# Attention scheduled by a planner: GpSimd shifts in half batches, other ring sizes, three-bank score phases

## The chip, the cores and the metric

One core of one Trainium2 chip. The metric is device time in microseconds of one execution; a run's time is the median of several executions. PE is TensorE, DVE VectorE, ACT ScalarE, POOL GpSimd, SP the queue that issues transfers.

## The reference, cut to what matters

```python
x = A_x                                   # 1 x 2048 x 512, bf16
xn = _layernorm(x)
# A: 32 query heads of 16, one key head and one value head
scores = einsum("bhqd,bkd->bhqk", q, k) * 16 ** -0.5
p = softmax(scores);  o = einsum("bhqk,bkd->bhqd", p, v);  s = o @ wo
# B: a gated layer
g = silu(silu(xn @ w1) @ w2)
return x + s * g
```

There are 32 x 2048 x 2048 scores. They come out of PE as 2,048 score slots of 128 keys x 512 queries, one PSUM bank each. Every slot must go through an exponential before PE multiplies it with the values.

## The kernel before

The kernel is a list scheduler. It simulates the five engines with planned durations, gives each engine a fixed order of instructions, and emits that order with semaphore waits. The chip may be late or early against the plan, but the order stays.

A slot leaves its bank in one of two ways. ACT takes it through `Exp`, one or two banks at a time. Or DVE takes it: four such slots make a *batch*. DVE writes each slot as a 16-bit integer whose bits, read as bf16, approximate the exponential (one *eviction*); then three *shifts* add a constant to the whole batch, and PE adds the four versions with different weights. A shift is an integer add from SBUF to SBUF: GpSimd does it, or, when many are open or a group of heads is closing, DVE.

PE alternates between *score phases* (tiles of 32 rows, two to four slots into two to four banks) and *column runs* (tiles of 32 columns: value products and the dense layers).

```python
T_P, T_SH, T_TR, T_AF = 600.0, 600.0, 630.0, 64.3      # planned ns; T_SH: a shift on Vector
T_P64, DV_MIN, T_LIB = 1035.0, 4, 300.0                # T_P64: a shift on GpSimd
...
NEAR, AHEAD = 24, 0.6
NPA, PRESS = 26, 20                                    # slots of the exp ring
WIDE, NMIN, EARLY = 2, 2, 200.0                        # NMIN: banks a score phase waits for
...
    def locked(self, eng, ports):                      # the planner's model of the shared port
        if ports != 2 or eng not in self.lock:
            return 0.0
        return self.lock[PO if eng == DV else DV]
...
    def run_engine(self, e, handle):                   # what is emitted: a fixed order with waits
        for op in self.order[e]:
            for d in op.waits:
                handle.wait_ge(d.sem, d.val)
            h = op.emit(handle)
...
    OB = 6
    BANKS = (0, 1, 2, 3, 4, 5, 7)
    NDB, NDS = 7, 6                                    # batch tiles, shift tiles
...
        def s_phase_ready():
            g = a_group(0)
            if g >= NG:
                return None
            if not all(slot_ok(g, i) for i in range(4) if left[g, i]):
                return None
            bt = bank_times()
            spare = JOB_SPARE if st["job"] < len(jobs) and not [a for a in active if not a.fixed] and jobs[st["job"]].pace <= progress() + 1e-9 else 0
            n = len(bt) - spare
            if n < 1:
                return None
            need = act_need() - 437.0
            n = min(n, 4)
            while n > NMIN and bt[n - 1][0] > need:
                n -= 1
            if n < NMIN and need > pl.clk[PE] or n < 1:
                return None
...
                bt.P[i] = pl.add(Task(DV, T_P, lambda v, b=b, i=i, bb=bt.b: v.tensor_scalar(
                    db_sb[:, bb, i * NQ:(i + 1) * NQ], bank(b), 128.0 * LOG2E, 128.0 * (SHIFT_BETA + 127.0),
                    op0=ALU.mult, op1=ALU.add), [("ps", b)], [("Db", bt.b, i)], 0, on_place=placed))
...
        def split(bt, s, j):
            whole = {}

            def placed(pop, eng):
                other = DV if eng == PO else PO
                pl.tasks[other].remove(whole[other])
                shifts.remove(whole)
                release(bt)
                for i in range(4):
                    kt = bt.slots[i]
                    pvq[bt.g][i].append((pop, v_lhs(j, bt.g, kt), ds_sb[:, s, i * NQ:(i + 1) * NQ].bitcast(BF16),
                                         [("Ds", s, i)] + v_reads(j, kt), ("s", s)))

            reads = [("Db", bt.b, i) for i in range(4)]
            step = int(SHIFT[j - 1])
            words = step | step << 16 | step << 32 | step << 48
            urgent = lambda: bt.g == st["gO"] and nleft[bt.g] <= CLOSING
            whole[DV] = pl.add(Task(DV, T_SH, lambda v: v.tensor_scalar(
                ds_sb[:, s, :], db_sb[:, bt.b, :], SHIFT[j - 1], 1.0, op0=ALU.add, op1=ALU.mult),
                reads, ds_keys(s), lambda: URGENT if urgent() else 6, list(bt.P.values()),
                on_place=lambda op: placed(op, DV), ports=2,
                gate=lambda: urgent() or len(shifts) >= DV_MIN))
            whole[PO] = pl.add(Task(PO, T_P64, lambda g: g.int64_add(
                ds_sb[:, s, :].bitcast(U64), db_sb[:, bt.b, :].bitcast(U64), words),
                reads, ds_keys(s), lambda: 5 if urgent() else 6, list(bt.P.values()),
                on_place=lambda op: placed(op, PO), ports=2))
            shifts.append(whole)
...
        # closing a group: the multiply with two SBUF inputs
            t3 = pl.add(Task(DV, 332.0, lambda v: v.tensor_tensor(
                o3[:, :, val:val + DH], f3[:, :, val:val + DH],
                rcp_sb[:, k, :].unsqueeze(2).to_broadcast([P, NQ // 32, DH]), ALU.mult),
                [("F", k), ("rcp", k)], [("otr", oi % 2, e)], 3, [t2, t2_task.get(oi - 2)], ports=2))
```

The softmax here doesn't subtract the row's maximum and nothing guards it: scores larger than these inputs give would overflow.

## Time and profile before

| | |
|---|---|
| time | 694.91 us (694.9 to 695.0) |
| span, granted TensorE clock | 693.2 us, 0.999 |
| GpSimd shifts, DVE shifts | 489 whole batches, 36 |
| PE's floor, PE's waiting | 656.3 us, 28.4 us |

A line of the groups reads: source line, engine, operation, output<-input, count | busy us, mean ns of one | idle time of the engine just before them, and what ended it. The timeline gives start, duration, engine, line, operation, count. Two figures come from the instruction order together with the starts in the trace: *PE's floor*, the sum over its phases and runs of what each takes from start to next start when nothing holds it, and *PE's waiting*, what it takes beyond that. The prediction shows how they come about.

### The profile page before, as it was taken

How to read it: one execution, taken by the hardware profiler on the slowest of the kernel's cores; microseconds unless marked ns; L12 is line 12 of the kernel's file. 1: busy time of each engine (PE TensorE's matmuls, PEld its weight loads, DVE VectorE, ACT ScalarE, POOL GpSimd, SP SyncE). 2: the span in 40 equal slices, each digit the busy share in tenths (PEclk: the TensorE clock that was granted, in tenths of full speed). 3: DMA queues.
4: the chain of work that ended last, by engine and by line, in shares of the span. 5: the costliest groups of instructions: out<-in, count | busy, mean ns of one | idle time of the engine just before them, and what ended most of it. 6: DMA issues, size and time to landing. Idle time of an engine off the chain costs nothing.

```text
span 693.2 us, 20821 instructions
## 1 busy us (share of the span) xinstructions
PE 670.8 (97%) x8843; PEld 193.8 (28%) x8843; DVE 627.9 (91%) x1088; ACT 667.4 (96%) x827; POOL 519.5 (75%) x500
## 2 busy tenths in 40 slices
PE   8899999999999999999999999999999999999995
PEld 4422222222222222222222222222222222222221
DVE  9889989989998999989998999989899988999994
ACT  4899999999999999999999999999999999999994
POOL 2067887797897778877698676788789677888891
PEclk9999999999999999999999999999999999999999
DMA  9310000000000000000000100000000000000000
GB/s 302 127 18 1 3 2 2 1 3 2 2 2 17 18 32 2 2 2 2 1 2 2 32 18 17 1 2 3 2 2 1 17 18 24 9 2 2 2 2 31
DMA packets 11435, 12.64 MB, mean 18 GB/s; under 512 B 1808, under 2 KB 10768, under 8 KB 11344
## 3 DMA queue, kind: packets, MB, share of 16 engines
q1 hardware_dynamic: 10288, 11.28, 5.1%
q8 instruction: 71, 1.16, 0.7%
q10 hardware_dynamic: 1056, 0.03, 0.1%
q14 instruction: 20, 0.16, 0.1%
HBM read 8.95 MB, written 2.10 MB: 16 GB/s over the span
## 4 chain that ended last, share of the span: by engine, by line
PE 62%; ACT 24%; DVE 12%; issue 1%; ACTq 0%; DVEq 0%
PE ps L1079 25%; ACT pa_sb L1341 23%; PE ps L776 21%; PE ps L466 15%; DVE db_sb L962 5%; DVE ds_sb L1014 2%; ACT t_sb L588 1%; DVE stats_sb L413 1%; DVE f_sb L1096 1%; DVE ob_sb L643 1%; DVE u_sb L590 0%; DVE otr_sb L1100 0%; DVE xn_sb L442 0%; DVE fin_sb L640 0%; DVE xnT_sb L493 0%
## 5 line engine op out<-in xcount | busy, mean ns | idle before, releaser
L1341 ACT ACTIVATE pa_sb<-ps 128x1024 bf16<-128x1024 f32 (+1 forms) x748 | 639.7, 980 | 7.4 <-PE ps L776 6.3
L1019 POOL INT64_ADD ds_sb<-db_sb x489 | 515.5, 1072 | 158.9 <-DVE db_sb L962 102.9
L962 DVE TENSOR_SCALAR db_sb<-ps 128x512 uint16<-128x512 f32 x700 | 449.9, 682 | 44.1 <-PE ps L776 40.0
L776 PE MATMUL ps<-qt_sb,kt_sb 32*128 32x512 bf16 x2048 | 257.4, 384 | 9.1 <-DVE db_sb L962 4.0
L1079 PE MATMUL ps<-ds_sb,v_sb 128*32 128x512 bf16 x2100 | 265.1, 383 | 0.2
L1079 PE MATMUL ps<-pa_sb,v_sb 128*32 128x512 bf16 x1348 | 242.8, 383 | 1.8 <-DVE ds_sb L1014 1.0
L1079 PE MATMUL ps<-db_sb,v_sb 128*32 128x512 bf16 x700 | 171.0, 383 | 2.8 <-DVE f_sb L1096 2.8
L776 PEld LDWEIGHTS ps<-qt_sb,kt_sb 32*128 32x128 bf16 x2048 | 63.9, 91 | 281.6 <-ACT pa_sb L1341 145.8
L1079 PEld LDWEIGHTS ps<-ds_sb,v_sb 128*32 128x32 bf16 x2100 | 65.9, 95 | 60.7 <-issue 40.0
L1079 PEld LDWEIGHTS ps<-pa_sb,v_sb 128*32 128x32 bf16 x1348 | 61.2, 95 | 45.1 <-issue 23.6
L466 PE MATMUL ps<-xnT_sb,w_sb 128*32 128x512 bf16 x896 | 73.1, 384 | 0.2 <-DVE db_sb L962 0.2
L466 PE MATMUL ps<-w_sb,u_sb 128*32 128x512 bf16 x896 | 69.6, 384 | 0.0
L1079 PEld LDWEIGHTS ps<-db_sb,v_sb 128*32 128x32 bf16 x700 | 42.6, 95 | 25.8 <-issue 13.3
L588 ACT ACTIVATE t_sb<-ps 128x512 bf16<-128x512 f32 x72 | 46.3, 643 | 0.0
L590 DVE SCALAR_TENSOR_TENSOR u_sb<-t_sb,ps 128x512 bf16<-128x512 bf16 x56 | 38.1, 681 | 4.5 <-ACT t_sb L588 4.0
L1014 DVE TENSOR_SCALAR ds_sb<-db_sb 128x2048 uint16<-128x2048 uint16 x36 | 37.3, 1039 | 0.1
L1096 DVE STREAM_TRANSPOSE f_sb<-ps 128x512 f32<-128x512 f32 x32 | 22.7, 708 | 7.5 <-PE ps L1079 7.4
L466 PEld LDWEIGHTS ps<-xnT_sb,w_sb 128*32 128x32 bf16 x896 | 16.7, 94 | 25.0 <-issue 18.3
L466 PEld LDWEIGHTS ps<-w_sb,u_sb 128*32 128x32 bf16 x896 | 16.2, 94 | 26.3 <-issue 22.8
L466 PE MATMUL ps<-wo_sb,on_sb 128*32 128x512 bf16 x256 | 20.4, 383 | 0.1
L466 PE MATMUL ps<-xnT_sb,wq_sb 128*32 128x512 bf16 x256 | 20.3, 383 | 0.0
L1100 DVE TENSOR_TENSOR otr_sb<-f_sb,rcp_sb 128x256 bf16<-128x256 f32 x32 | 19.0, 595 | 0.2
(53 smaller groups left out, 153.3 us busy)
## 6 DMA issues: line engine op xcount, KB each, us to landing
w_sb<-in_B_w_dram SPq DMA_DIRECT2D x2, 1792.0 KB, 13.1
xr_sb<-in_A_x_dram SPq DMA_DIRECT2D x16, 128.0 KB, 2.6
out_dram<-ob_sb SPq DMA_DIRECT2D x16, 128.0 KB, 1.7
ds_sb<-in_A_x_dram SPq DMA_DIRECT2D x3, 512.0 KB, 7.2
ds_sb<-in_A_x_dram SPq DMA_DIRECT2D x4, 128.0 KB, 2.6
wq_sb<-in_A_wq_dram SPq DMA_DIRECT2D x1, 512.0 KB, 5.2
wo_sb<-in_A_wo_dram SPq DMA_DIRECT2D x1, 512.0 KB, 16.0
kt_sb<-kt_sb SPq DMA_DIRECT2D x4, 64.0 KB, 2.3
```

The source lines that it names most:

```text
L413: ts_ = pl.add(Task(DV, 593.0, lambda v, t=t: v.bn_stats(stats_sb[:, t, :], x_tile(t)), [xkey(t)], [("st", t)], 1 + j, gate=(lambda: q_don ...
L466: last = h.matmul(bank(b)[32 * j:32 * (j + 1), 0:n], lhsT=lhs(j), rhs=rhs, start=start, stop=stop, tile_position=(0, 32 * j), skip_group_c ...
L588: t1 = Task(AC, 490.0, lambda a: a.activation(t_sb[:, k, :], src, ACT.Tanh, scale=scale), [held], [("t", k)], 0, [t0])
L590: t2 = Task(DV, T_P, lambda v: v.scalar_tensor_tensor(out=dst, in0=t_sb[:, k, :], scalar=1.0, in1=src, op0=ALU.add, op1=ALU.mult), [held, ...
L776: return pe.matmul(bank(b), lhsT=kt_sb[32 * i:32 * i + 32, g % 2, kt * P:(kt + 1) * P], rhs=qt_sb[32 * i:32 * i + 32, (g // 2) % NQR, :], ...
L962: bt.P[i] = pl.add(Task(DV, T_P, lambda v, b=b, i=i, bb=bt.b: v.tensor_scalar(db_sb[:, bb, i * NQ:(i + 1) * NQ], bank(b), 128.0 * LOG2E, 1 ...
L1014: whole[DV] = pl.add(Task(DV, T_SH, lambda v: v.tensor_scalar(ds_sb[:, s, :], db_sb[:, bt.b, :], SHIFT[j - 1], 1.0, op0=ALU.add, op1=ALU.m ...
L1019: whole[PO] = pl.add(Task(PO, T_P64, lambda g: g.int64_add(ds_sb[:, s, :].bitcast(U64), db_sb[:, bt.b, :].bitcast(U64), words), reads, ds_ ...
L1079: h = pe.matmul(bank(OB)[32 * i:32 * (i + 1), :], lhsT=lhs, rhs=rhs, start=s0, stop=s1, tile_position=(0, 32 * i), skip_group_check=True)
L1096: t1 = pl.add(Task(DV, T_TR, lambda v: v.transpose(f_sb[:, k, :], bank(OB)), [("ps", OB)], [("F", k)], 1, [norm.get(("m", g - 2))]))
L1100: t3 = pl.add(Task(DV, 332.0, lambda v: v.tensor_tensor(o3[:, :, val:val + DH], f3[:, :, val:val + DH], rcp_sb[:, k, :].unsqueeze(2).to_br ...
L1341: op = pl.place(AC, 0.8333 * NQ * n + T_AF, lambda a: a.activation(pa_sb[:, s * NQ:(s + n) * NQ].rearrange("p (b n) -> p b n", n=NQ), ps3[ ...
```

## The change

It means to feed PE more evenly. GpSimd's adds are cut into halves of two slots, so that PE can start on the first half earlier; the shift ring grows from 6 to 8 tiles, and the exp ring shrinks from 26 to 22 slots (its limit `PRESS` from 20 to 16) and the batch ring from 7 to 6 tiles to pay for it; a phase waits for three banks and takes no two slots in one row group (the 32 rows of PE that a slot's tile uses). `NEAR`, below called the *closing limit*, falls from 24 to 12: with no more value products than that still to do, a group counts as closing. The planned 545 ns for a half add stands in `T_P64`. The source line numbers of the changed kernel are higher by 3 to 14: L1019 becomes L1032, L1014 L1026, L1100 L1114, L1341 L1355.

```diff
--- before.py
+++ after.py
@@ -20,7 +20,8 @@
 
 
 T_P, T_SH, T_TR, T_AF = 600.0, 600.0, 630.0, 64.3
-T_P64, DV_MIN, T_LIB = 1035.0, 4, 300.0
+T_P64, DV_MIN, T_LIB = 545.0, 4, 300.0
+NPIECE = 2
 RSQRT_M = float(0x5F1FFFF9)
 RSQRT_C = ((-0.703952253, 0.703952253 * 2.38924456), (-0.5, 1.5))
 
@@ -37,7 +38,7 @@
 ENGINES = (PE, AC, DV, PO, SP)
 MM = 216.0
 BLG = 0
-NEAR, AHEAD = 24, 0.6
+NEAR, AHEAD = 12, 0.6
 SWITCH, SKEW = 105.0, 10.0
 INF = float("inf")
 DVE_LIMIT = 4000.0
@@ -48,10 +49,12 @@
 LOW_USE, HIGH_USE, USE_WIN = 0.55, 0.8, 3000.0
 S_TOL = 30.0
 CLOSING, URGENT = 3, 1.5
-NPA, PRESS = 26, 20
+NPA, PRESS = 22, 16
+NDB, NDS = 6, 8
+STOL4 = 0.0
 START_Z, START_H = 8, 14
 EVAC = ()
-WIDE, NMIN, EARLY = 2, 2, 200.0
+WIDE, NMIN, EARLY = 2, 3, 200.0
 ONE_LIMIT = 2500.0
 A_LOW, JOB_SPARE = 1000.0, 0
 
@@ -293,7 +296,7 @@
 
     OB = 6
     BANKS = (0, 1, 2, 3, 4, 5, 7)
-    NDB, NDS = 7, 6
+
     NQR, NON = 4, 2 * NOC
 
     with ExitStack() as es:
@@ -809,28 +812,28 @@
             if not free:
                 return None
             bt = Job()
-            bt.g, bt.slots, bt.b, bt.P, bt.nsh, bt.left = g, {}, free[0], {}, 0, K + 3
+            bt.g, bt.slots, bt.b, bt.P, bt.nsh, bt.left = g, {}, free[0], {}, 0, 4 * K
             return bt
 
         def pick_a(n, avoid):
             res = []
-            used = set()
+            used = set(avoid)
             g = a_group(0)
             st["gA"] = g
-            for gg in (g, g + 1):
-                if gg >= NG:
-                    break
-                order = sorted(range(4), key=lambda i: (i in avoid and gg == g, -a_left(gg, i), i))
-                again = True
-                while len(res) < n and again:
-                    again = False
-                    for i in order:
-                        if len(res) < n and a_left(gg, i) > 0 and (i not in used or len(used) == 4 or gg == g and nleft[gg] <= 4):
-                            if not slot_ok(gg, i):
-                                return None if not res else res
-                            res.append((gg, i, take(gg, i)))
-                            used.add(i)
-                            again = True
+            for strict in (True, False):
+                for gg in (g, g + 1):
+                    if gg >= NG:
+                        break
+                    again = True
+                    while len(res) < n and again:
+                        again = False
+                        for i in sorted(range(4), key=lambda i: (-a_left(gg, i), i)):
+                            if len(res) < n and a_left(gg, i) > 0 and (i not in used or not strict and not res):
+                                if not slot_ok(gg, i):
+                                    return None if not res else res
+                                res.append((gg, i, take(gg, i)))
+                                used.add(i)
+                                again = True
             return res
 
         class Unit:
@@ -852,7 +855,7 @@
                 return None
             need = act_need() - 437.0
             n = min(n, 4)
-            while n > NMIN and bt[n - 1][0] > need:
+            while n > NMIN and bt[n - 1][0] > need + STOL4:
                 n -= 1
             if n < NMIN and need > pl.clk[PE] or n < 1:
                 return None
@@ -992,20 +995,29 @@
 
         shifts = []
 
-        shifts = []
-
         def split(bt, s, j):
-            whole = {}
-
-            def placed(pop, eng):
-                other = DV if eng == PO else PO
-                pl.tasks[other].remove(whole[other])
-                shifts.remove(whole)
-                release(bt)
-                for i in range(4):
+            whole = {"po": []}
+            width = 4 // NPIECE
+
+            def ready(pop, slots):
+                for i in slots:
+                    release(bt)
                     kt = bt.slots[i]
                     pvq[bt.g][i].append((pop, v_lhs(j, bt.g, kt), ds_sb[:, s, i * NQ:(i + 1) * NQ].bitcast(BF16),
                                          [("Ds", s, i)] + v_reads(j, kt), ("s", s)))
+
+            def placed_dv(pop):
+                for t in whole["po"]:
+                    pl.tasks[PO].remove(t)
+                shifts.remove(whole)
+                ready(pop, range(4))
+
+            def placed_po(pop, k):
+                if whole[DV] is not None:
+                    pl.tasks[DV].remove(whole[DV])
+                    whole[DV] = None
+                    shifts.remove(whole)
+                ready(pop, range(k * width, (k + 1) * width))
 
             reads = [("Db", bt.b, i) for i in range(4)]
             step = int(SHIFT[j - 1])
@@ -1014,12 +1026,14 @@
             whole[DV] = pl.add(Task(DV, T_SH, lambda v: v.tensor_scalar(
                 ds_sb[:, s, :], db_sb[:, bt.b, :], SHIFT[j - 1], 1.0, op0=ALU.add, op1=ALU.mult),
                 reads, ds_keys(s), lambda: URGENT if urgent() else 6, list(bt.P.values()),
-                on_place=lambda op: placed(op, DV), ports=2,
-                gate=lambda: urgent() or len(shifts) >= DV_MIN))
-            whole[PO] = pl.add(Task(PO, T_P64, lambda g: g.int64_add(
-                ds_sb[:, s, :].bitcast(U64), db_sb[:, bt.b, :].bitcast(U64), words),
-                reads, ds_keys(s), lambda: 5 if urgent() else 6, list(bt.P.values()),
-                on_place=lambda op: placed(op, PO), ports=2))
+                on_place=placed_dv, ports=2, gate=lambda: urgent() or len(shifts) >= DV_MIN))
+            for k in range(NPIECE):
+                cols = slice(k * width * NQ, (k + 1) * width * NQ)
+                whole["po"].append(pl.add(Task(PO, T_P64, lambda g, cols=cols: g.int64_add(
+                    ds_sb[:, s, cols].bitcast(U64), db_sb[:, bt.b, cols].bitcast(U64), words),
+                    reads[k * width:(k + 1) * width], ds_keys(s)[k * width:(k + 1) * width],
+                    lambda: 5 if urgent() else 6, list(bt.P.values()),
+                    on_place=lambda op, k=k: placed_po(op, k), ports=2)))
             shifts.append(whole)
 
         x_free = [False]
```

## The prediction

> **What bounds the kernel now.** I read the page first. Its busy shares put three engines near the end of their time:
>
> ```profile
> PE 670.8 (97%) x8843; PEld 193.8 (28%) x8843; DVE 627.9 (91%) x1088; ACT 667.4 (96%) x827; POOL 519.5 (75%) x500
> ...
> PE 62%; ACT 24%; DVE 12%; issue 1%; ACTq 0%; DVEq 0%
> ```
>
> PE and ACT are both "full", and the chain that ended last runs through PE for 62% of the span and through ACT for 24%. But busy is no measure of work, because a record that overlaps its neighbour is busy whether or not the engine waited inside. So I looked next at starts, in the timeline. ACT alone:
>
> ```profile
> 301.65 15.93 ACT L1341 ACTIVATE pa_sb<-ps 128x1024 bf16<-128x1024 f32 x17
> 317.44 0.63 ACT L588 ACTIVATE t_sb<-ps 128x512 bf16<-128x512 f32 x1
> 317.92 2.90 ACT L1341 ACTIVATE pa_sb<-ps 128x1024 bf16<-128x1024 f32 x3
> ```
>
> 17 exps of two banks take 15.79 us to the next start: 0.929 each. Over the trace, start to next start, a two-bank exp needs 0.904 at least and a one-bank activation 0.477. ACT's least work is therefore 600 x 0.904 + 148 x 0.477 + 72 x 0.477 (the gates) = 647.3 us; it actually spreads over 670.0. ACT has 22.7 us of hidden waiting although its row says 96%. Now PE:
>
> ```profile
> 310.55 0.39 PE L776 MATMUL ps<-qt_sb,kt_sb 32*128 32x512 bf16 x3
> 310.87 0.61 PE L466 MATMUL ps<-w_sb,u_sb 128*32 128x512 bf16 x8
> 311.42 0.39 PE L776 MATMUL ps<-qt_sb,kt_sb 32*128 32x512 bf16 x3
> 311.74 0.62 PE L466 MATMUL ps<-w_sb,u_sb 128*32 128x512 bf16 x8
> ```
>
> The reader is to see the alternation: a score phase (32-row tiles) of three slots lasts 0.32 us to the next start, whatever its slots (medians 0.318, 0.321, 0.325 for two, three, four), and a run of column-tiled matmuls 0.55 for 8, 0.764 for 12, 0.980 for 16: 0.216 for each round of four and 0.116 once. The instruction order gives the counts: 649 score phases (101 of two slots, 347 of three, 198 of four, three odd ones), 643 column runs with 1,677 rounds. PE's floor: phases 211.8; runs 643 x 0.116 + 1,677 x 0.216 less 2.8 for half-wide fillers = 434.0; full-array prologue 10.5; together 656.3 us. The time is then 2.3 (before the first matmul) + 656.3 + 28.4 (PE waiting) + 6.2 (after the last) + 1.7 (measured time over span) = 694.9. PE is the bound; of its 28.4 us of waiting 11.0 lie in the first 50 us and the last 20, and 17.4 between (13.9 a phase waiting for a bank, 3.5 a run waiting for an operand).
>
> ```profile
> PEld ps L776 <- ACT pa_sb L1341: 145.8, 348, 0.8
> PEld ps L776 <- DVE db_sb L962: 104.1, 227, 1.2
> ...
> PEld ps L1079 <- POOL ds_sb L1019: 12.1, 53, 0.4
> ```
>
> These waits name who frees the banks: ACT most often, DVE next; GpSimd's shifts hardly hold anything. Weight loads run ahead of matmuls, so most of these sums is not lost time. Where PE really waits, the chain in order of time shows a group being closed on DVE:
>
> ```profile
> 152.02 0.73 DVE f_sb L1096
> ...
> 153.06 0.80 DVE otr_sb L1100
> 153.85 1.44 DVE ds_sb L1014
> 155.30 0.62 DVE on_sb L1107
> 155.92 0.59 DVE db_sb L962
> ```
>
> An urgent shift of 1.44 us and a normalising multiply of 0.80 stand in front of the eviction that PE needs. The groups:
>
> ```profile
> L1019 POOL INT64_ADD ds_sb<-db_sb x489 | 515.5, 1072 | 158.9 <-DVE db_sb L962 102.9 <-PE ps L1079 55.2
> L962 DVE TENSOR_SCALAR db_sb<-ps 128x512 uint16<-128x512 f32 x700 | 449.9, 682 | 44.1 <-PE ps L776 40.0 <-POOL ds_sb L1019 0.4
> L1014 DVE TENSOR_SCALAR ds_sb<-db_sb 128x2048 uint16<-128x2048 uint16 x36 | 37.3, 1039 | 0.1
> L1100 DVE TENSOR_TENSOR otr_sb<-f_sb,rcp_sb 128x256 bf16<-128x256 f32 x32 | 19.0, 595 | 0.2
> ```
>
> **What the Trainium skill says.** SBUF — State Buffer, Who interferes with whom: a Vector instruction in a 2-port mode, or with two SBUF inputs, and a GpSimd instruction exclude each other for the whole instruction; the second blocks fully. The trace agrees: the same DVE shift takes 683 ns at its shortest and 1,602 at its longest, the multiply 415 and 1,256, the excess being near one GpSimd add (1,015 start to start, 1,039 alone). TensorEngine Tiling (Array Packing), Key Properties: changing the tiling mode drains the engine; agrees, as 0.105 and 0.116 us above the streaming time per change. ScalarE: Activation LUTs, What ACT_TABLE_LOAD costs: 0.833 ns per element plus a fixed part. Agrees: (904 - 477)/512 = 0.834, and 50 ns fixed from start to start. GPSIMD Engine Reference, Instruction dispatch: each instruction pays tens of cycles of software dispatch. A half add therefore costs somewhat more than half; no row of this kernel shows it.
>
> **The change part by part.** The order of instructions of both kernels:
> - *Batches.* 180 instead of 175 batches of four slots go to DVE plus shifts; ACT loses 20 slots: 600 -> 632 two-bank exps, 148 -> 64 single ones. ACT's floor: 632 x 0.904 + 136 x 0.477 = 636.2, that is -11.1. Each moved slot needs four value matmuls instead of one: +60, or 15 rounds; fillers +16.
> - *Phases.* 648 instead of 649, but 549 of three and 97 of four; none of two. So asking for three banks saves no changes of mode: the twos vanish together with half of the fours. It makes each phase one pair for ACT and one slot for DVE, which is why single exps vanish. Phases with two slots in a row group (0.533 instead of 0.321): 14 before, two after. Phases in all: 208.8, -2.9.
> - *Rounds.* 1,682 against 1,677: 19 more by matmul count, but 14 fewer wasted on partly filled rounds. Runs: 644 x 0.116 + 1,682 x 0.216 - 3.2 = 434.8, +0.8. PE's floor: 654.1, -2.2.
> - *DVE.* +20 evictions x 0.643 = +12.9; shifts 36 -> 15, -21 x 1.036 = -21.8. The wait for GpSimd, on average 0.36 for a shift (1,039 - 683) and 0.18 for a multiply (595 - 415), should halve with adds of half length: 15 x 0.18 + 32 x 0.09 = -5.6. DVE: about -14.
> - *GpSimd.* 489 whole adds become 1,050 halves. The changed kernel plans 545 ns for one; its old plan of 1,035 for a whole was right within 0.5% of the trace, so I take 545: 572 us in the 639 us in which GpSimd has work, 90% instead of 78%. It lies beside PE's work.
> - *Rings.* Exp ring 26 -> 22 slots, shift ring 6 -> 8 tiles: less cushion between exp and PE, more between shifts and PE. I count nothing for either.
>
> What reaches PE: floor -2.2. Of the 17.4 us of waiting in the middle: the chain has 1.7% = 11.8 us on DVE shifts, 21/36 of that is 6.9, and I count half as real, -3.5, since the chain then moves to PE; half of the lock's 5.6, -2.8. I add 1.5 for tighter shift supply and 0.5 for the start, where the fillers hint at more idle. Sum: 2.3 + 654.1 + 11.5 + (17.4 - 3.5 - 2.8 + 1.5 = 12.6) + 6.2 + 1.7 = 688.4 us, -0.9%.
>
> **The rivals.** (1) *ACT is the bound.* For: 96% busy, and it holds most banks. Then the time falls by ACT's 11.1 to 683.8, more if singles wasted more. Against: its own 22.7 us of hidden waiting, and PE's floor 9 us above its own before and 18 after. (2) *GpSimd becomes the bound.* The smallest add on the page's engine (one word, at load) took 189 ns; a line through it and 1,039 gives a half at 613, less 24 of overlap 589, and 1,050 x 0.589 = 618 us of 639: shifts late, runs waiting for operands, 695 to 712. Against: a first call is likely dearer than the rest. (3) *All waiting in the middle goes,* since phases become regular: 675.8. Against: closing a group still needs its transpose before the next group's values can start, 32 times. (4) *Three banks come later than two:* PE holds phases back with a smaller exp ring, waiting stays at 17.4 or grows by 5: 693 to 698.
>
> **Range and chances.** Rival 1 or half of rival 3 gives the low end, 682.5; rival 4 the high, 696. Faster by over 2% (below 681.0) asks for two thirds of the middle's waiting to go: 0.10. Slower by over 2% (above 708.8) asks for rival 2 in full: 0.04. Else 0.86.
>
> **What would show it.** Right: score phases near 0.321 and runs of 8 at 0.548 as before; two-bank exps at 0.904 or above with ACT's share of busy falling; the DVE shift's mean below 900 and the multiply's below 530; GpSimd's mean near 545 and some 85 to 92% busy; PE waiting between 50 and 670 us near 12. Wrong: GpSimd above 580 and 95% busy with PE waiting for shifts; PE waiting unchanged (the DVE closings did not matter); or a total below 682 with waiting under 6 (regularity mattered most).

## The result, and the profile after

The changed kernel takes **737.57 us** (737.42 to 737.76, four executions) against 694.94 us for the kernel before in the same rounds: 1.0613 times as long (95% interval 1.0595 to 1.0632). A ratio is the mean time of one kernel's fast runs over that of the other's of the same rounds, so not quite the ratio of the medians. The prediction of 688.4 us, and its range, were wrong.

First the page of the changed kernel, its busy shares and the chain by engine, then the row of the granted TensorE clock in 40 slices, then what the cores view says of clock and span:

```profile
PE 683.9 (93%) x8919; PEld 195.0 (26%) x8919; DVE 659.9 (90%) x1087; ACT 662.5 (90%) x775; POOL 632.1 (86%) x1061
...
PE 47%; ACT 26%; DVE 21%; issue 3%; DMA 1%; POOL 0%; SPq 0%; ACTq 0%; DVEq 0%
```

```profile
PEclk9999999999999999998998999989989999989999
```

```profile
core 0: 736.0 us, clock 0.968
```

PE and ACT lose share, DVE's part of the chain grows from 12% to 21%, and, what no row of the kernel before hinted at, the clock is below full in several slices. In the clock records it is at one half in eight stretches of 3.4 or 6.8 us, 44.4 us in all, the first 50 us and the tail after the last matmul left out. The kernel before has none there.

The groups, each shape apart:

```profile
L1032 POOL INT64_ADD ds_sb<-db_sb x1050 | 628.2, 621 | 90.9 <-DVE db_sb L965 61.2 <-PE ps L1093 28.7
...
L1114 DVE TENSOR_TENSOR otr_sb<-f_sb,rcp_sb 128x256 bf16<-128x256 f32 x32 | 42.5, 1329 | 0.1
...
L1026 DVE TENSOR_SCALAR ds_sb<-db_sb 128x2048 uint16<-128x2048 uint16 x15 | 26.0, 1735 | 0.0
```

A half add takes 621 ns (587 from start to start), not 545. And the two DVE instructions that share a port with GpSimd, which were to wait half as long, wait far longer: the multiply 1,329 on average against 595, the shift 1,735 against 1,039. What the views by tile and line give as least, median and longest, for the multiply before and after, then for the shift after:

```profile
L1100 DVE TENSOR_TENSOR otr_sb<-f_sb,rcp_sb x32: 415/434/1256, 50.2 to 685.3; 128x256 bf16<-128x256 f32 x32
```

```profile
L1114 DVE TENSOR_TENSOR otr_sb<-f_sb,rcp_sb x32: 409/714/6111, 59.6 to 728.1; 128x256 bf16<-128x256 f32 x32
```

```profile
L1026 DVE TENSOR_SCALAR ds_sb<-db_sb x15: 685/1053/6436, 42.5 to 718.6; 128x2048 uint16<-128x2048 uint16 x15
```

The medians are harmless. A few instructions take 2.5 to 6.4 us. One of them in the timelines of DVE, GpSimd, PE and ACT:

```profile
337.79 5.18 DVE L1114 TENSOR_TENSOR otr_sb<-f_sb,rcp_sb 128x256 bf16<-128x256 f32 x1
342.90 0.68 DVE L965 TENSOR_SCALAR db_sb<-ps 128x512 uint16<-128x512 f32 x1
```

```profile
336.80 5.90 POOL L1032 INT64_ADD ds_sb<-db_sb  x10
```

```profile
343.72 0.61 PE L779 MATMUL ps<-qt_sb,kt_sb 32*128 32x512 bf16 x3 [4.31 <-DVE db_sb L965]
344.26 0.62 PE L469 MATMUL ps<-xnT_sb,wq_sb 128*32 128x512 bf16 x4
```

```profile
344.38 1.02 ACT L1355 ACTIVATE pa_sb<-ps 128x1024 bf16<-128x1024 f32 x1 [4.34 <-PE ps L779]
```

The multiply starts at 337.79 while GpSimd is in a run of 48 adds without a pause, in the course of the 40th; the line of GpSimd shows the last ten. It ends at 342.97, just after the last of them, at 342.70. Behind it, in DVE's order, stands the eviction that frees PE's bank: PE idles 4.31 us, ACT 4.34. And PE comes back slow: 0.54 us from the start of the score phase to the next run, where 0.32 was the rule. The windows around it (columns: length, then busy us of PE, its weight loads, DVE, ACT and GpSimd, then the granted clock) show this:

```profile
335.00:339.00 4.00, 3.96 (x56) 1.04 (x57) 4.00 (x6) 3.90 (x5) 4.00 (x8) 1.00 0.02 4
339.00:343.70 4.70, 0.41 (x8) 0.01 (x1) 4.70 (x3) 1.03 (x2) 3.70 (x7) 0.73 0.00 0
343.70:350.00 6.30, 6.28 (x61) 1.35 (x61) 5.11 (x9) 4.21 (x5) 4.01 (x7) 0.66 0.00 0
```

Of the numbers after the stretch the fourth is DVE's busy time: DVE is "busy" all through its wait, which is why its 90% tells nothing.

Sorted by size, PE's waiting of 72.8 us in the changed kernel is: 10.7 at the two ends, 34.4 in ten stalls of over 1 us, 15.6 in the stretches at half clock, and 12.2 in everything else. Nine of the ten stalls begin within some 2 us of one of the nine DVE instructions that take over 2 us, and each of these nine ends within 0.6 us after the last add of a run. The waits say the same, and that shifts coming late to PE are not it (12.1 us before, 13.4 after):

```profile
PE ps L779 <- DVE db_sb L965: 36.3, 20, 5.1
...
PEld ps L1093 <- POOL ds_sb L1032: 13.4, 57, 0.5
```

### The profile page after: what moved, and what is told of

Same layout as the page of the kernel before. It is cut to its first block, busy times and chain, and to the rows that moved or that the text cites. A ratio compares the mean times of both kernels' runs of the same rounds, so it can differ in the third digit from the quotient of the medians.

```text
span 736.0 us, 21675 instructions
## 1 busy us (share of the span) xinstructions
PE 683.9 (93%) x8919; PEld 195.0 (26%) x8919; DVE 659.9 (90%) x1087; ACT 662.5 (90%) x775; POOL 632.1 (86%) x1061
## 4 chain that ended last, share of the span: by engine, by line
PE 47%; ACT 26%; DVE 21%; issue 3%; DMA 1%; POOL 0%; SPq 0%; ACTq 0%; DVEq 0%
ACT pa_sb L1355 25%; PE ps L1093 19%; PE ps L779 17%; PE ps L469 11%; DVE db_sb L965 11%; DVE otr_sb L1114 3%; DVE ds_sb L1026 2%; ACT t_sb L591 2%; DVE u_sb L593 1%; DMA ds_sb<-in_A_x_dram 1%; DVE stats_sb L416 1%; DVE f_sb L1110 1%; DVE ob_sb L646 0%; POOL ds_sb L1032 0%; SPq L363 0%
## 5 line engine op out<-in xcount | busy, mean ns | idle before, releaser
L1032 POOL INT64_ADD ds_sb<-db_sb x1050 | 628.2, 621 | 90.9 <-DVE db_sb L965 61.2
L1355 ACT ACTIVATE pa_sb<-ps 128x1024 bf16<-128x1024 f32 (+1 forms) x696 | 632.4, 998 | 54.9 <-PE ps L779 52.9
L965 DVE TENSOR_SCALAR db_sb<-ps 128x512 uint16<-128x512 f32 x720 | 468.9, 682 | 57.7 <-PE ps L779 54.0
L1093 PE MATMUL ps<-ds_sb,v_sb 128*32 128x512 bf16 x2160 | 280.0, 392 | 0.0
L1093 PE MATMUL ps<-db_sb,v_sb 128*32 128x512 bf16 x720 | 182.5, 389 | 0.8 <-DVE f_sb L1110 0.6
L1093 PEld LDWEIGHTS ps<-ds_sb,v_sb 128*32 128x32 bf16 x2160 | 70.9, 96 | 64.6 <-issue 42.8
L469 PE MATMUL ps<-w_sb,u_sb 128*32 128x512 bf16 x896 | 75.7, 397 | 0.0
L1093 PEld LDWEIGHTS ps<-db_sb,v_sb 128*32 128x32 bf16 x720 | 45.1, 96 | 22.2 <-issue 13.4
L591 ACT ACTIVATE t_sb<-ps 128x512 bf16<-128x512 f32 x72 | 43.7, 607 | 0.2 <-PE ps L469 0.2
L1114 DVE TENSOR_TENSOR otr_sb<-f_sb,rcp_sb 128x256 bf16<-128x256 f32 x32 | 42.5, 1329 | 0.1
L1026 DVE TENSOR_SCALAR ds_sb<-db_sb 128x2048 uint16<-128x2048 uint16 x15 | 26.0, 1735 | 0.0
```

Of the source, the lines that this page charges most:

```text
L469: last = h.matmul(bank(b)[32 * j:32 * (j + 1), 0:n], lhsT=lhs(j), rhs=rhs, start=start, stop=stop, tile_position=(0, 32 * j), skip_group_c ...
L591: t1 = Task(AC, 490.0, lambda a: a.activation(t_sb[:, k, :], src, ACT.Tanh, scale=scale), [held], [("t", k)], 0, [t0])
L1032: whole["po"].append(pl.add(Task(PO, T_P64, lambda g, cols=cols: g.int64_add(ds_sb[:, s, cols].bitcast(U64), db_sb[:, bt.b, cols].bitcast( ...
L1093: h = pe.matmul(bank(OB)[32 * i:32 * (i + 1), :], lhsT=lhs, rhs=rhs, start=s0, stop=s1, tile_position=(0, 32 * i), skip_group_check=True)
L1114: t3 = pl.add(Task(DV, 332.0, lambda v: v.tensor_tensor(o3[:, :, val:val + DH], f3[:, :, val:val + DH], rcp_sb[:, k, :].unsqueeze(2).to_br ...
L1355: op = pl.place(AC, 0.8333 * NQ * n + T_AF, lambda a: a.activation(pa_sb[:, s * NQ:(s + n) * NQ].rearrange("p (b n) -> p b n", n=NQ), ps3[ ...
```

## The experiments

Three theories. **A**, the starved port: when GpSimd's adds follow one another without a pause for long, a DVE instruction that needs the shared port is not let in at the end of an add but waits for the end of the run. The halves bring long runs because they are planned too short: GpSimd falls behind, finds all its inputs ready, and never pauses. **B**, GpSimd's throughput: 1,050 x 0.587 is 616 us of work, and that alone makes everything late. **C**, the rings or the rules for phases cost the time.

"Waits over 2 us" below counts the multiplies, the shifts and the residual sums on DVE. The "longest run" is of adds each of which starts before the record of the one before it ends. It goes on when a DVE instruction was let in between two adds. "Half clock" leaves out the first 50 us and the tail after the last matmul.

| kernel | time us | ratio | GpSimd adds | longest run | waits over 2 us | half clock us | PE floor | PE waiting |
|---|---|---|---|---|---|---|---|---|
| before | 694.9 | 1 | 489 whole | 18 | 0 | 0 | 656.3 | 28.4 |
| the change | 737.6 | 1.0613 | 1,050 half | 62 | 9 | 44.4 | 654.1 | 72.8 |
| e1 pause every 8 | 702.6 | 1.0105 | 1,050 half | 8 | 0 | 6.8 | 654.1 | 37.6 |
| e7 pause every 24 | 709.9 | 1.0186 | 1,050 half | 24 | 3 | 17.1 | 654.1 | 44.8 |
| e5 wait, no pause | 735.7 | 1.0579 | 1,050 half | 70 | 8 | 44.4 | 654.1 | 71.2 |
| e2 planned at 600 | 707.2 | 1.0183 | 984 half | 40 | 3 | 13.7 | 652.7 | 48.4 |
| e6 both | 697.5 | 1.0030 | 984 half | 8 | 0 | 0 | 652.7 | 34.1 |
| e4 halves alone | 711.1 | 1.0230 | 936 half | 61 | 1 | 6.8 | 657.8 | 42.4 |
| e3 all but halves | 692.8 | 0.9964 | 524 whole | 15 | 0 | 0 | 654.7 | 26.3 |
| e8 phase rules alone | 694.0 | 0.9982 | 502 whole | 16 | 0 | 0 | 649.6 | 32.7 |
| e9 rings alone | 693.8 | 0.9975 | 502 whole | 18 | 0 | 0 | 661.4 | 21.6 |
| e10 e3 with 24 exp slots | 688.4 | 0.9906 | 522 whole | 25 | 1 | 3.4 | 650.6 | 26.4 |

All these results are correct ones. The floor, the waiting, the runs and the waits are of the one profiled execution of each kernel; e2's took 711.8 us, the longest of its four.

### e1: a pause at every eighth add

The order of every engine is that of the changed kernel; one wait is added to every eighth add.

```diff
     def finalize(self, new_sem):
+        adds = self.order[PO]
+        for k in range(len(adds) - 1, 12, -EVERY):       # EVERY = 8
+            adds[k].deps.append(adds[k - 1])
         for e in ENGINES:
```

> The changed kernel, same order on every engine; only every eighth GpSimd add also waits for the end of the add before it (131 breaks). Theory A (starved port: in long unbroken runs of adds a Vector instruction with two SBUF inputs or in a 2-port mode does not get the port and waits 2 to 6 us): those waits fall below 2 us at most, the mean of the normalising multiply from 1,329 to below 700 ns, and the time falls to 700 to 718 us although GpSimd has some 15 us more to do. Theory B (GpSimd's throughput alone, 1,050 adds at 0.586): the time stays or rises, 735 to 755. Theory C (the rings and phase rules are what costs): no change, 733 to 742.

Measured: 702.63 us (702.35 to 702.95), interval of the ratio 1.009 to 1.012. The groups of this kernel (its lines are four higher):

```profile
L1036 POOL INT64_ADD ds_sb<-db_sb x1050 | 632.0, 622 | 52.1 <-DVE db_sb L969 38.0 <-PE ps L1097 1.2
...
L1118 DVE TENSOR_TENSOR otr_sb<-f_sb,rcp_sb 128x256 bf16<-128x256 f32 x32 | 19.7, 616 | 0.1
...
L1030 DVE TENSOR_SCALAR ds_sb<-db_sb 128x2048 uint16<-128x2048 uint16 x15 | 14.3, 952 | 0.0
```

GpSimd has the same adds of the same length plus 131 pauses, so more to do, and the kernel is 35 us faster. The multiply's mean is 616 instead of 1,329, with 894 at most. A holds; B as the main cause falls. What remains above the kernel before looks like B's share, though no run takes it apart: PE waits 25.8 us for GpSimd's shifts in the weight loads' row of the waits (13.4 in the changed kernel), and DVE's evictions wait 5.8 us (0.4) for batch tiles that late adds still read:

```profile
PEld ps L1097 <- POOL ds_sb L1036: 25.8, 83, 1.5
...
DVE db_sb L969 <- POOL ds_sb L1036: 5.8, 9, 2.7
```

### e5: as many waits, but no pause

```diff
-            adds[k].deps.append(adds[k - 1])
+            adds[k].deps.append(adds[k - 4])
```

> As e1_break8, with as many waits at the same adds, but each for the add four before, which is long done: a wait without a pause. If the pause is what lets the Vector engine in (theory A), nothing is gained: 730 to 745 us and waits of over 4 us. If it is the waiting instruction as such that opens the port, 700 to 708 as e1_break8.

Measured: 735.66 us (731.75 to 739.91), ratio 1.0579 (1.0533 to 1.0624). The groups:

```profile
L1036 POOL INT64_ADD ds_sb<-db_sb x1050 | 629.4, 620 | 88.1 <-DVE db_sb L969 64.0 <-PE ps L1097 23.3
...
L1118 DVE TENSOR_TENSOR otr_sb<-f_sb,rcp_sb 128x256 bf16<-128x256 f32 x32 | 46.2, 1443 | 0.1
```

Not the wait as an instruction opens the port but the gap it makes when its add has not yet ended. The longest multiply takes 6,164 ns, as in the changed kernel.

### e7: a pause at every 24th add

The edit is that of e1 with `EVERY = 24`.

> As e1_break8 with a pause at every 24th add. In the changed kernel the Vector engine lost from about the 12th add of a run on, so A expects it between: 708 to 728 us, longest wait at the port 3 to 6 us but fewer of them than the nine over 2 us of the changed kernel. B: 730 to 742.

Measured: 709.90 us (705.16 to 710.21), ratio 1.0186 (1.0148 to 1.0225). Between e1 and the changed kernel, with three waits over 2 us, the longest 4,049 ns. The dose works in the right direction.

### m1 and m2: the port by itself

Two measuring kernels write zeros. Their outputs are wrong, which doesn't matter for the times. Each was executed once. GpSimd issues a run of adds with no wait inside; one DVE instruction waits for the n-th add of the run and then needs the port.

```diff
+for i in range(total):                        # GpSimd: 48 adds of 256 words or 36 of 512
+    g.int64_add(dst[...], src[...], 1).then_inc(sp, 1)
...
+v.wait_ge(sp, base + p)                       # DVE: released by the p-th add
+v.tensor_tensor(vc[:], va[:], vb[:], ALU.add).then_inc(sv, 1)
```

> A measurement alone, with a wrong result on purpose (it writes zeros). First GpSimd adds of 32, 64, 128, 256 and 512 eight-byte words, ten each: I expect start to start a straight line with 0.586 us at 256 and 1.015 at 512, so some 0.157 fixed and 1.68 ns a word. Then unbroken runs of 48 half adds or 36 whole adds, and one Vector instruction (a sum of two SBUF inputs, or a 16-bit shift in a 2-port mode) released by the 2nd, 5th, 8th, 12th, 16th, 24th or 32nd add of the run, twice each. Theory A as I hold it (adds that follow one another without a pause let the Vector instruction in only while the run is young, whatever their size): released by the 2nd or 5th it waits one or two adds, released by the 24th or 32nd it waits to the end of the run, 5 us or more, with halves and with wholes. Theory A2 (only short adds starve it): with wholes it waits at most two adds at any place. Theory A3 (it takes a loaded memory or something else of the kernel): at most two adds everywhere.

The length of an add, start to start, from m1's trace (medians of nine; a word is 8 bytes):

| words | 32 | 64 | 128 | 256 (half) | 512 (whole) |
|---|---|---|---|---|---|
| ns | 211 | 268 | 375 | 588 | 1,015 |

That is (1,015 - 211) / 480 = 1.675 ns a word and 158 ns for each instruction. Two halves cost 2 x 588 - 1,015 = 161 ns more than a whole. The 545 in the plan was too low, and the prediction's "proportional plus a little" with it; the straight line of the prediction's second rival gave 589.

How long the sum of two SBUF inputs took on DVE, released by the p-th add (both trials agree within 7 ns, but for the whole adds at 32, whose second trial started later and took 3.8):

| released by add | 2 | 5 | 8 | 12 | 16 | 24 | 32 |
|---|---|---|---|---|---|---|---|
| halves, us | 0.76 | 0.76 | 0.76 | 0.76 | 0.76 | 14.29 | 9.58 |
| wholes, us | 1.19 | 1.19 | 1.19 | 1.19 | 1.19 | 12.35 | 4.23 |

The 16-bit shift on DVE behaves the same (1.03 and 1.45 up to the 16th; 14.56 and 12.62 at the 24th). Early in a run DVE waits for one add; late in a run it waits for the end of the run. Wholes starve it as halves do, and with nothing else running, so A2 and A3 fall.

> A measurement alone, with a wrong result on purpose. Runs of 48 adds of 256 or 128 words and a Vector sum of two SBUF inputs released by the 15th to the 24th add. From m1 the Vector engine loses from some add between the 17th and the 24th on; if the number of adds counts and not their time, the edge is at the same number for both sizes; if time counts (between 9.4 and 14.1 us), the short adds still let it in at the 24th. Two Vector instructions, at the 12th and again at the 24th to 36th: if a granted port starts the count afresh, the second waits one add when it comes within some 20 adds of the first, so at the 24th and 28th, not at the 36th. A pause (wait for the add just before) in front of the 17th: arrivals at the 20th to 30th wait one add, that at the 42nd may lose again. A wait for a long-done add at the same place: as without, so the 24th and 30th lose.

m2 puts the arrivals closer. Its DVE timeline: released by the 15th, 16th, 17th and 18th half add of 48, then by the 15th and 16th of 48 adds of 128 words:

```profile
17.18 0.75 DVE L70 TENSOR_TENSOR vc_sb<-va_sb,vb_sb 128x512 bf16<-128x512 bf16 x1 [9.36 <-POOL dst_sb L81]
46.28 19.00 DVE L70 TENSOR_TENSOR vc_sb<-va_sb,vb_sb 128x512 bf16<-128x512 bf16 x1 [28.35 <-POOL dst_sb L81]
75.58 18.41 DVE L70 TENSOR_TENSOR vc_sb<-va_sb,vb_sb 128x512 bf16<-128x512 bf16 x1 [10.30 <-POOL dst_sb L81]
104.88 17.82 DVE L70 TENSOR_TENSOR vc_sb<-va_sb,vb_sb 128x512 bf16<-128x512 bf16 x1 [10.89 <-POOL dst_sb L81]
...
301.20 0.55 DVE L70 TENSOR_TENSOR vc_sb<-va_sb,vb_sb 128x512 bf16<-128x512 bf16 x1 [5.93 <-POOL dst_sb L81]
319.86 8.52 DVE L70 TENSOR_TENSOR vc_sb<-va_sb,vb_sb 128x512 bf16<-128x512 bf16 x1 [18.11 <-POOL dst_sb L81]
```

The edge is sharp and lies at the same place for both sizes, between the 15th and the 16th add here and past the 16th in m1: it is the number of adds that counts, not their time. So cutting the adds brings the edge nearer in time: 16 halves take 9.4 us, 16 wholes 16.2. A grant starts the count afresh: after one at the 12th, arrivals at the 24th and 28th take 0.76 us, those at the 32nd and 36th 9.58 and 6.82. So does a pause in front of the 17th add (a gap of 97 ns in the records): arrivals at the 20th, 24th and 30th take 0.76, those at the 36th and 42nd 7.23 and 3.70. A wait for a long-done add at the same place does nothing: 16.64, 14.29 and 10.76 us at the 20th, 24th and 30th. Released by the 20th, with the pause and with the idle wait:

```profile
606.20 0.76 DVE L70 TENSOR_TENSOR vc_sb<-va_sb,vb_sb 128x512 bf16<-128x512 bf16 x1 [12.19 <-POOL dst_sb L81]
...
749.67 16.64 DVE L70 TENSOR_TENSOR vc_sb<-va_sb,vb_sb 128x512 bf16<-128x512 bf16 x1 [12.07 <-POOL dst_sb L81]
```

The expectation that a second arrival would be let in within "some 20 adds" was close: the edge lies between 16 and 20 adds after the first. One thing does not fit a wait to the end of the run: behind adds of 128 words the starved instruction got in at about the 38th or 39th of 48. That is left open, and so is the mechanism that makes the edge.

The traces of the twelve kernels above show the same edge under load. Take every multiply, shift and residual sum that came in a run with at least three adds still to follow, and count the adds since the last pause or since the last of these instructions was let in, the add then running included. Of the 304 that came by the 17th add, none took over 1 us more than its shortest time in the kernel before; of the 39 that came at the 18th or later, 25 did. All 25 instructions of over 2 us in these kernels came at the 18th or later and ended within 0.6 us after the run's last add. This is also why e4 has a run of 61 and only one such wait: instructions let in on the way started the count again.

### e2 and e6: an honest plan, without and with pauses

```diff
-T_P64, DV_MIN, T_LIB = 545.0, 4, 300.0
+T_P64, DV_MIN, T_LIB = 600.0, 4, 300.0
```

e6 adds the edit of e1 to it.

> The changed kernel, scheduled with 600 ns for a half add in place of 545, so that the plan is honest about the 586 measured: 984 half adds and 33 Vector shifts instead of 1,050 and 15. A and B: GpSimd keeps up and pauses again, 688 to 700 us, longest wait of a Vector shift or multiply below 2 us. C: the rings and phase rules are still there, so above 710.

> The honest plan of e2 with the pauses of e1. A: no wait at the port over 2 us, PE's waiting near the 26 to 30 us of the kernels with whole adds, 690 to 697 us. B: the pauses cost GpSimd 14 us, so no better than e2's 707.

Measured: e2 707.20 us (706.11 to 711.82), ratio 1.0183 (1.0147 to 1.022), which misses A's expectation of 688 to 700; e6 697.54 us (697.25 to 698.12), ratio 1.003 (1.0015 to 1.0045), just above A's 697, with 34.1 us of waiting where A expected 26 to 30. B's expectation for e6 fails too: the pauses gained. In e2 GpSimd still makes runs of up to 40 adds, and three DVE instructions wait over 2 us, the longest 4,502 ns. So being on plan does not by itself break the runs. The four times make a table: with the plan of 545, 737.6 without pauses and 702.6 with them; with 600, 707.2 and 697.5. The pauses are worth 35.0 and 9.7 us, the plan 30.4 and 5.1 (the other plan also brings another order and 18 more shifts on DVE). The two overlap: a GpSimd that is behind pauses less by itself.

### e3 and e4: the halves against the rest

e3 takes the change with whole adds; e4 takes the halves, planned at 545, into the old rings, rules and limits.

```diff
 e3, against the change
-T_P64, DV_MIN, T_LIB = 545.0, 4, 300.0
-NPIECE = 2
+T_P64, DV_MIN, T_LIB = 1035.0, 4, 300.0
+NPIECE = 1
 e4, against the change (and the old choice of slots for ACT)
-NEAR, AHEAD = 12, 0.6
+NEAR, AHEAD = 24, 0.6
-NPA, PRESS = 22, 16
-NDB, NDS = 6, 8
+NPA, PRESS = 26, 20
+NDB, NDS = 7, 6
-WIDE, NMIN, EARLY = 2, 3, 200.0
+WIDE, NMIN, EARLY = 2, 2, 200.0
```

> All of the change but the halves: whole adds (planned at 1,035), 524 of them, 13 Vector shifts, new rings, row-group rule and three-bank phases. A and B: 684 to 694 us, since a whole add is planned right. C: above 710.

> Only the half adds (planned at 545), with the old rings, the old choice of slots, two-bank phases and the old closing limit: 936 half adds, 48 Vector shifts. A and B: GpSimd falls behind its plan by 936 x 0.041 = 38 us less its slack, so slow, 705 to 735 us, with waits of over 2 us of Vector instructions at the port in A. C: 692 to 698, as before the change.

Measured: e3 692.79 us (691.84 to 693.92), ratio 0.9964 (0.9948 to 0.998); e4 711.08 us (710.33 to 712.56), ratio 1.023 (1.021 to 1.0249). C falls: the rest of the change is slightly good. The halves alone cost 16 us, less than the 45 between e3 and the whole change, where the plan puts 1,050 of them on GpSimd instead of 936; whether that number makes the difference was not tested. In e4 only one DVE instruction waited over 2 us (5,000 ns), which suggests that a larger part of e4's loss is lateness (B) than in the whole change; it was not separated.

### e8, e9 and e10: the rest taken apart, and a better kernel

e8 has of e3 only the phase rules, e9 only the rings and the closing limit. e10 is e3 with

```diff
-NPA, PRESS = 22, 16
+NPA, PRESS = 24, 18
```

> Of e3, only the phase rules (three banks, no two slots of a phase in one row group) with whole adds and the old rings and closing limit. Its PE floor by the cost per phase and round is 649.6, 6.7 below the kernel before. If waiting stays near 28, 688 to 691; if the floor is reached by phases that come late, waiting grows and it stays at 693 to 697.

> Of e3, only the rings (22 exp slots, 8 shift tiles, 6 batches) and the closing limit, with whole adds and the old phase rules. PE floor 661.4, 5.2 above the kernel before, so 697 to 702 if waiting stays near 28; 692 to 696 if the longer shift ring takes waiting away.

> A try for a better kernel, not a test of the theories: e3 (whole adds, the new phase rules and shift ring) with 24 exp slots and a limit of 18 in place of 22 and 16. Its PE floor is 650.6, against 654.7 of e3 and 656.3 of the kernel before. With e3's 26 of waiting 688 to 690; if waiting rises to e8's 33, 694 to 696. No wait at the port over 2 us.

Measured: e8 694.02 us, ratio 0.9982 (0.9965 to 0.9999); e9 693.83 us, 0.9975 (0.996 to 0.999); e10 688.44 us, 0.9906 (0.9889 to 0.9922). In e8 the floor falls by 6.7 and waiting grows by 4.3; in e9 the floor rises by 5.1 and waiting falls by 6.8. Phases of at least three save PE's changes of mode (631 phases against 649) but come later; the other rings and the closing limit, which were not tested apart, take waiting away. e10 gets both in part: 639 phases, floor 650.6, waiting 26.4. It is the fastest kernel of this study, 7.0 us under the kernel before, and, against its expectation, it still has one multiply of 3.4 us in a run of 25 whole adds. That its time equals the number predicted for the change is chance.

## Why the prediction was wrong

By its own steps:

- *PE is the bound, with a floor of 654.1 us after the change.* Right as far as it goes: phases of three start to next start at 0.321 and runs of 8 at 0.548 in their medians, as before. It was PE that paid for every stall.
- *Waiting in the middle 12.6, at the ends 11.5.* The ordinary waiting, without stalls of over 1 us and half-clock stretches, came to 12.2 and 10.7. The four terms that made up the 12.6 were not tested one by one, and one of them has the wrong sign, so this agreement shows only that nothing else went wrong.
- *"I take 545".* The mis-sized term. A half add takes 587 in the kernel and 588 by itself; 1,050 of them are 616 us, not 572. The prediction had the right figure, 589, in its second rival and set it aside because "a first call is likely dearer than the rest". The one word at load was no dearer: m1's line gives 158 + 1.7 = 160 ns start to start, some 185 with the overlap of 25, against the 189 of the record.
- *"The wait for GpSimd ... should halve".* The step that failed, and the largest error. The reasoning was one add at most per wait, from a kernel before in which no unbroken run was longer than 18 adds. The planner's own model of the port assumes the same: the later of the two waits for the end of one instruction. In the changed kernel, runs reach 62. What the three kinds of DVE instruction take beyond their shortest grew from 20.6 us to 49.3 instead of shrinking by 5.6, and nine of them hold everything behind them in DVE's order.
- *GpSimd "lies beside PE's work".* It does not where it holds a port that DVE needs while DVE holds banks that PE needs.
- *The clock* was in no step. In or after eight of the stalls, of 2 to 5 us, PE runs at half clock for 3.4 or 6.8 us; this is 15.6 us of waiting on top of the stalls' 34.4. Together they are 50.0, and 688.4 + 50.0 - 0.4 - 0.8 (the two kinds of ordinary waiting, below their estimates) is 737.2.
- *Rival 2* named the right engine and the right length but the wrong way: runs of matmuls do not wait for shifts, phases wait for evictions behind a starved DVE instruction. Its 695 to 712 is what e1, e2 and e7 show, where most of the starving is gone.

## What to carry to other kernels

When two engines share a port, look at the longest wait of the instructions that need it and at how long the other engine runs without a pause, not at means: here cutting an instruction in two did not halve the wait but lengthened it. A pause, a wait for the instruction just before, at every eighth GpSimd add gave 35 us back on balance, although it made the shifts themselves later. In a schedule fixed by planned durations, measure each new shape by itself first: an engine that is 8% behind its plan finds more of its inputs ready and loses pauses on which others had relied. An honest plan alone did not bring enough of them back (e2).

## What the Trainium skill lacked or had wrong

- SBUF — State Buffer, Who interferes with whom: it says that whoever issues first has the shared pair "for the whole instruction". It lacks what happens over a run: released by up to the 15th or 16th add of a run without a pause, DVE waits for one add (0.76 us behind halves); from the next on (from the 24th at the latest with adds of 512 words) it waits to the end of the run, through 4 to 32 adds (3.7 to 19.0 us), but for the adds of 128 words, where it got in some 9 adds before the end. A gap of 97 ns or a grant starts the count again.
- The same section: "Issue order, not op shape, decides who blocks." The runs agree as to the size of the adds (the same edge for 128 and 256 words) but not as to order: a DVE instruction whose record starts over 30 adds before that of a GpSimd add got the port after it.
- GPSIMD Engine Reference, Instruction dispatch: it gives "tens of cycles" per instruction for the dispatcher's call. For this add the fixed part is 158 ns from start to start, and a word of 8 bytes takes 1.675 ns; no page has this instruction's time.
- TensorE: Matmul & The Clock Gate, Part 1: it describes a half-rate clock after an idle window of about 3.4 us. The trace agrees as to the rate and the length: eight stretches at 0.5 of 3.4 or 6.8 us. It does not show that PE must idle for 3.4 us: half clock followed a stall of 2.0 us (433.3), began 1.8 us into one of 4.3 (341.2), and did not follow one of 3.1 (at 216.6). What the page says could have been used, and the prediction did not.
- ScalarE: Activation LUTs, What ACT_TABLE_LOAD costs: it gives an overlap of about 93 ns for activations back to back. Two-bank exps from PSUM take 1,017 ns where they follow closest, 904 from start to start: an overlap of 113.
